# Output projection moved into the token tiles of the spectral layer, tokens handed over in SBUF

## Chip, cores and metric

The kernel runs on one core of a Trainium2 chip. Its time is the device time of the whole program in microseconds. The kernel before takes 1611.79 us, the median of three runs (1611.19 to 1612.21).

## What is computed

x is [2048, 576] in float32. Four layers follow one another, each with a layer norm over the features and a residual: attention (A), spectral (B), A, B.

```
def _A_ref(x, wqkv, wo):          # H = 32 heads of 18, window W = 256
    q, k, v = qkv[0], qkv[1], qkv[2]              # from x @ wqkv
    scores = einsum("bhqd,bhkd->bhqk", q, k) * (Dh ** -0.5)
    p = softmax(where(0 <= i - j < W, scores, -1e9))
    return merge_heads(p @ v) @ wo                # the output projection
def _B_ref(x, w_r, w_i):
    return irfft2(rfft2(x) * (w_r + 1j * w_i))
x = x + _A_ref(_layernorm(x), wqkv, wo)
x = x + _B_ref(_layernorm(x), w_r, w_i)           # and both once more
```

## The kernel before, in words

The program is written out in the order in which each engine runs it; there is no scheduler. Every engine, and SP as the main DMA queue, goes through its own instructions in order and waits on semaphores. Numbers are kept as a high and a low part, so that a product is three matmuls (high by high, low by high, high by low).

**Layer A** (`layer_a`, L433) has a first stage over 16 token tiles (norm, transposes, v) and a second one over 128 steps: 8 groups of 4 heads by 16 query tiles. In step t the scores are multiplied (E, L661), ACT takes the exponentials (L662), POOL masks them (L664, L667), and two steps later the products with v go to a PSUM bank U (`pv`, L677). After four query tiles U is copied by ACT (L682), and `norm` (L684) transposes it, divides by the row sums on DVE (L690, L692) and stores 72 features of 512 tokens to the DRAM tensor `o_d` (L693, SP).

The output projection is done in the same loop, from step OB = 120 on, one tile of 128 neighbouring tokens a step: `o_load` (L729) reads o and x, `o_tail` (L733) splits the last 64 features on POOL, `o_turn` (L736) makes five transposes and splits the result on ACT and DVE, `o_unit` (L748) makes 28 matmuls of 288 columns (14 steps by two halves), adds x on DVE, stores the new token rows (L760), takes the mean and variance on DVE (L764 to L766) and stores those as well (`mv_d`, L767). Tiles 0 to 6 lie between the last attention steps, the rest follow. `o_room` (L712) puts the weights `wo` and these tiles into the space of the attention's inputs, which are done by then.

**Layer B** (`layer_b`, L98) begins by reading `mv_d` back (L122) and taking 1/sqrt for all tokens (L136 to L138), makes an identity, and loads the tokens in pairs of tiles (`ld`, L111) and the constants dc and gc (L118, L119). A token tile is strided here: tile n2 holds the tokens 16 p + n2 for the partitions p. The first stage is `pipe(NT, ...)` (L239), which staggers these functions over the 16 tiles: `f0` (L166: xn on ACT, its even and odd parts eo and the small tile tl on POOL), `f1` (L189: six transposes into the PSUM tile tp, split into et by ACT and DVE), `f2` (L202: 14 matmuls of 290 columns with dc, PSUM tile pf, split into yh and yl), `f3` (L217: 12 matmuls with gc, PSUM tile pz, copied to ye and stored to the DRAM tensor yd). In a step f1 is for the tile after that of f2, and f3 for the tile before. Loads for later stages go out on the way: fc, m2 and w in `pre` (L155), ic (128 x 12 x 290) and ga (128 x 1024) in f0 of tile 8 (L168, L169).

The next stage reads yd crosswise, a group g at a time (`g0`, L241), so it needs all of the first stage. The first group is put together in SBUF from the stored tiles and, for the last three tiles (FD = 13), from ye directly (L228 to L235). `g1m` (L253, matmuls p) and `g2` (L271, matmuls pq) follow, then a second exchange, and the last stage (`i0`, `i1`, `i2`, from L304; matmuls pi and po), which reads the tokens again for the residual and stores the layer's result.

Of the kernel before, what the change touches and what calls it, by code (L numbers as in the profile page):

```python
# [17 lines left out]
NF = 290  # L18
# [79 lines left out]
def layer_b(tc, src, dst, mv_d, dc_d, ic_d, fc_d, gc_d, ga_d, m2_d, w_d, dram):  # L98
# [6 lines left out]
    with tc.tile_pool(name="bc", bufs=1) as cp, tc.tile_pool(name="bw", bufs=2) as wp, \  # L105
# [4 lines left out]

        def ld(n2, h):  # L111
            if n2 % 2 == 0:
                x = wp.tile([128, 2, D], F32, tag="x", name=f"x{n2}", bufs=4)
# [3 lines left out]
            if n2 == 0 and not ys:  # L117
                nc.sync.dma_start(dc.bitcast(F32), dc_d.bitcast(F32))  # L118
                nc.sync.dma_start(gc.rearrange("p a j b c -> p (a j b c)").bitcast(F32), gc_d.bitcast(F32))  # L119

        mv = cp.tile([128, NT, 2], F32, name="mv")
        nc.sync.dma_start(mv.rearrange("p a b -> p (a b)"), mv_d.rearrange("(p n) e -> p (n e)", n=NT))  # L122
        eps = cp.tile([128, 1], F32, name="eps"); V.memset(eps, 1e-5)

        A.activation(cp.tile([128, 1], F32, name="se"), eps, AF.Sqrt)
        ident = cp.tile([128, 128], F32, name="ident")
        make_identity(nc, ident)
        dc = cp.tile([128, 10, NF], F32R, name="dc")
        gc = cp.tile([128, 2, 2, 2, 128], F32R, name="gc")
        ga = cp.tile([128, 2, 2, 256], F32R, name="ga")  # L130
        fc = cp.tile([128, 16, 2, 2, 64], F32, name="fc")
        m2 = cp.tile([128, 16, 2, 128], F32, name="m2")
        ic = cp.tile([128, 12, NF], F32R, name="ic")
        rs = cp.tile([128, NT], F32, name="rs")
        nb = cp.tile([128, NT], F32, name="nb")
        A.activation(rs, mv[:, :, 1], AF.Sqrt, bias=eps)  # L136
        V.reciprocal(rs, rs)
        V.scalar_tensor_tensor(nb, mv[:, :, 0], -1.0, rs, op0=ALU.mult, op1=ALU.mult)  # L138
        zs, eos = [], []
# [13 lines left out]
        NW = 7  # L153
# [12 lines left out]
        def f0(n2, h):  # L166
            if n2 == 8:
                nc.sync.dma_start(ic.bitcast(F32), ic_d.bitcast(F32))  # L168
                nc.sync.dma_start(ga.rearrange("p a j c -> p (a j c)").bitcast(F32), ga_d.bitcast(F32))  # L169
            if n2 == 6:  # L170
                for j in range(3):
                    z = cp.tile([128, 2, 2, 354], F32R, name=f"zs{j}")
                    V.memset(z.bitcast(F32)[:, :, :, 289:320], 0.0)
                    zs.append(z)
            x = xs[n2]
            xn = wp.tile([128, D], F32, tag="ta", name=f"xn{n2}", bufs=3)
            A.activation(xn, x, AF.Identity, bias=nb[:, n2:n2 + 1], scale=rs[:, n2:n2 + 1])
            eo = h["eo"] = eos[n2 % 4]
            P.tensor_add(eo[:, 0, 1:288], xn[:, 1:288], xn[:, 575:288:-1])
            A.copy(eo[:, 0, 0:289:288], xn[:, 0:289:288])  # L180
            (V if n2 < 2 else P).tensor_sub(eo[:, 1, 0:287], xn[:, 1:288], xn[:, 575:288:-1])

            tl = h["tl"] = wp.tile([128, 2, 3, 33], F32, tag="td", name=f"tl{n2}", bufs=3)
            e = eo[:, :, 256:289]
            P.tensor_copy(tl[:, :, 0].bitcast(F32R), e)
            P.tensor_copy(tl[:, :, 2].bitcast(F32R), e)
            P.tensor_sub(tl[:, :, 1].bitcast(F32R), e, tl[:, :, 0])
# [14 lines left out]
        def f2(n2, h):  # L202
            ps = pp.tile([128, 2, 512], F32, tag="mm", name=f"pf{n2}", bufs=3)
            et = h["et"]
            for c in range(2):
# [3 lines left out]
                for q, (si, mi) in enumerate(seq):  # L209
                    T.matmul(o, et[:, c, si], dc[:, b + mi], start=q == 0, stop=False)  # L210
                T.matmul(o, et[0:99, c, 4], dc[0:99, b + 4], start=False, stop=True)
# [5 lines left out]
        def f3(n2, h):  # L217
# [10 lines left out]
            if n2 == FD:  # L228
                y = wp.tile([128, 2, 2, NF], F32, tag="x", name="y0", bufs=4)
                nc.sync.dma_start(y[0:8 * FD].rearrange("p a c f -> p a (c f)"), yd[0][0:2, 0:FD].rearrange("a n i f -> (n i) a f"))  # L230
                for q in range(2):
                    ys[q] = y[:, q]
# [6 lines left out]
        pipe(NT, [(0, ld), (5, lambda n2, h: n2 or f2(n2, h)), (4, f1), (5, lambda n2, h: n2 and f2(n2, h)), (6, f3), (2, f0)])  # L239

        def g0(g, h):  # L241
            if g % 2 == 0 and g not in ys:
                y = wp.tile([128, 2, 2, NF], F32, tag="x", name=f"y{g}", bufs=4)
                nc.sync.dma_start(y.rearrange("p a c f -> p a (c f)"), yd[0][g:g + 2].rearrange("a n i f -> (n i) a f"))
                for q in range(2):
                    ys[g + q] = y[:, q]
# [6 lines left out]
        def g1m(g, h):  # L253
# [6 lines left out]
            p1 = wp.tile([128, 2, NF], F32, tag="tw", name=f"p1_{g}")  # L260
# [10 lines left out]
        def g2(g, h):  # L271
# [9 lines left out]
            if g == FD:  # L281
                for n2 in range(2):
                    y = ys["i", n2] = wp.tile([128, 2, NF], F32, tag="y", name=f"yi{n2}", bufs=4)
# [10 lines left out]
        pipe(16, [(0, g0), (9, g2), (7, g1m), (2, gw)])  # L294

        def ly(n2, h):
# [4 lines left out]
            y = h["y"] = wp.tile([128, 2, NF], F32, tag="y", name=f"yi{n2}", bufs=4)  # L301
# [32 lines left out]
        def i2(n2, h):  # L334
# [14 lines left out]
            bs = wp.tile([128, NF], F32, tag="td", name=f"bs{n2}", bufs=3)  # L349
# [10 lines left out]
NQ = 8  # L360
# [72 lines left out]
def layer_a(tc, src, dst, mv_d, wqk_d, wv_d, wo_d, dram, copy, wvs, second):  # L433
# [5 lines left out]
    o_d = dram.tile([S, D], F32, name="o_d")  # L439
    with ExitStack() as ctx:  # L440
# [115 lines left out]
        with ExitStack() as c2:  # L556
# [127 lines left out]
            def norm(n, c):  # L684
# [8 lines left out]
                nc.sync.dma_start(o_d[c * 512:(c + 1) * 512, 72 * n:72 * n + 72].rearrange("(a p) e -> p a e", a=4), o)  # L693
# [16 lines left out]
            ob = {}  # L710

            def o_room():  # L712
                for r, parts in ((bp.tile([128, 5 * S], F32R, tag="xh", name="oroom"), (("wh", 1, 5 * D), ("wl", 1, 5 * D), ("oT", 3, 9 * 128))),
                                 (bp.tile([128, 4 * S], F32, tag="xl", name="ofree"), (("x", 6, D), ("o", 4, D), ("tl", 4, 128)))):
                    at = 0
                    for nm, n, w in parts:
                        ob[nm] = [r[:, at + k * w:at + k * w + w] for k in range(n)]
                        at += n * w
                ob["raw"] = r[:, 0:5 * D]
                for a, b in ((0, 2), (2, 5)):  # L720
                    nc.sync.dma_start(ob["raw"][:, a * D:b * D], wo_d[:, a * D:b * D])

            def o_split(k):
                c = slice(k * D, k * D + D)
                raw = ob["raw"][:, c]
                A.copy(ob["wh"][0][:, c], raw)
                P.tensor_sub(ob["wl"][0][:, c], raw, ob["wh"][0][:, c].bitcast(F32))

            def o_load(u):  # L729
                nc.sync.dma_start(ob["o"][u % 4], o_d[u * 128:(u + 1) * 128])  # L730
                nc.sync.dma_start(ob["x"][u % 6], src[u * 128:(u + 1) * 128])

            def o_tail(u):  # L733
                tail_split(nc, ob["tl"][u % 4], ob["o"][u % 4][:, 512:576])

            def o_turn(u):  # L736
                o, tl = ob["o"][u % 4], ob["tl"][u % 4]
                oT = ob["oT"][u % 3]
                tp = pp.tile([128, 512], F32, tag="S", name=f"tpa{u}", bufs=3)
                for kt in range(4):  # L740
                    T.transpose(tp[:, kt * 128:kt * 128 + 128], o[:, kt * 128:kt * 128 + 128], ident)
                tq = pp.tile([128, 512], F32, tag="S", name=f"tpb{u}", bufs=3)
                T.transpose(tq[:, 0:128], tl, ident)
                A.copy(oT[:, 0:512], tp)
                V.tensor_sub(oT[:, 512:1024], tp, oT[:, 0:512].bitcast(F32))
                A.copy(oT[:, 1024:1152], tq[:, 0:128])

            def o_unit(u):  # L748
                oT = ob["oT"][u % 3]
                ps = [pp.tile([128, 512], F32, tag="E" if u > 4 and u % 2 else "pj", name=f"ops{u}_{n}", bufs=2) for n in range(2)]  # L750
                ks = k_steps()
                for i, (wk, p, xk) in enumerate(ks):
                    w = ob["wh" if p == "h" else "wl"][0]
                    for n in range(2):
                        T.matmul(ps[n][:, 0:288], oT[:, xk * 128:xk * 128 + 128], w[:, wk * D + n * 288:wk * D + n * 288 + 288],  # L755
                                 start=i == 0, stop=i == len(ks) - 1)
                x = ob["x"][u % 6]
                for n in range(2):
                    V.tensor_add(x[:, n * 288:n * 288 + 288], x[:, n * 288:n * 288 + 288], ps[n][:, 0:288])
                nc.sync.dma_start(dst[u * 128:(u + 1) * 128], x)  # L760

                st = wp.tile([128, 2, 6], F32, tag="st", name=f"ost{u}", bufs=2)
# [88 lines left out]
```

## Time and profile before

| | |
|---|---|
| time of the profiled execution | 1608.87 us |
| its span | 1607.2 us |
| mean TensorE clock granted | 0.97 |
| matmul windows at 590 to 603 us: PE busy | 0.42 of 13 us |
| DMA moved | 277.96 MB, mean 173 GB/s |

How it is read: PE is TensorE's matmuls, PEld its weight loads, DVE is VectorE, ACT ScalarE, POOL GpSimd, SP the DMA queue of SyncE. A line such as L755 is a line of the kernel before. Rows of groups have the operation, output and inputs by the program's names, the count, then busy time, the mean in ns, and the idle time before with what ended it. Rows of the timeline have start, length, engine, line and operation. The chain of work is followed back from the last instruction. PEclk is the share of the full clock that TensorE was granted. Two layers of each kind run, so each hand-over from A to B occurs twice, at about 590 and 1390 us.

### The profile page before, as it was taken

How to read it: one execution, taken by the hardware profiler on the slowest of the kernel's cores; microseconds unless marked ns; L12 is line 12 of the kernel's file. 1: busy time of each engine (PE TensorE's matmuls, PEld its weight loads, DVE VectorE, ACT ScalarE, POOL GpSimd, SP SyncE). 2: the span in 40 equal slices, each digit the busy share in tenths (PEclk: the TensorE clock that was granted, in tenths of full speed). 3: DMA queues.
4: the chain of work that ended last, by engine and by line, in shares of the span. 5: the costliest groups of instructions: out<-in, count | busy, mean ns of one | idle time of the engine just before them, and what ended most of it. 6: DMA issues, size and time to landing. Idle time of an engine off the chain costs nothing.

```text
span 1607.2 us, 38259 instructions
## 1 busy us (share of the span) xinstructions
PE 1507.2 (94%) x13872; PEld 1146.1 (71%) x13872; DVE 961.1 (60%) x3047; ACT 811.0 (50%) x1876; POOL 623.8 (39%) x1030
## 2 busy tenths in 40 slices
PE   7999999999999969998979999999999999799898
PEld 7975666666656968848979756666666569698498
DVE  4337777777774444456743377777777745444566
ACT  5524666666667115424445246666666671153244
POOL 2172334444445105352411723444343451153534
PEclk9999999999999988998979999999999999899989
DMA  6656446455543856866474564454434438678673
GB/s 194 181 180 200 145 149 184 151 167 151 155 133 98 165 160 239 285 216 215 149 231 116 177 204 149 142 156 140 140 120 148 135 100 168 180 246 277 209 227 135
DMA packets 189385, 277.96 MB, mean 173 GB/s; under 512 B 87566, under 2 KB 88590, under 8 KB 188174
## 3 DMA queue, kind: packets, MB, share of 16 engines
q1 hardware_dynamic: 180878, 255.54, 53.1%
q10 hardware_dynamic: 7680, 15.59, 2.9%
q0 software_dynamic: 640, 4.39, 1.0%
q8 instruction: 111, 1.82, 0.5%
q14 instruction: 76, 0.62, 0.1%
HBM read 176.47 MB, written 102.32 MB: 173 GB/s over the span
## 4 chain that ended last, share of the span: by engine, by line
PE 83%; DMA 4%; POOL 2%; ACT 2%; DVE 2%; issue 1%; SPq 1%; POOLq 0%; ACTq 0%; DVEq 0%
PE pj L588 15%; PE E L661 14%; PE U L677 12%; PE ops L755 7%; PE S L629 6%; PE pi L322 5%; PE vps L546 4%; PE pf L210 4%; PE pz L223 3%; PE po L343 3%; PE tpo L687 2%; PE p L258 1%; DMA yd<-ze 1%; PE pq L277 1%; PE po L347 1%
## 5 line engine op out<-in xcount | busy, mean ns | idle before, releaser
L631 DVE CUSTOM_DVE_ANT_0 jk<-S,mask 128x384 bf16<-128x384 f32 (+2 forms) x1024 | 500.2, 529 | 151.3 <-PE S L629 139.0
L662 ACT ACTIVATE P<-E 128x384 f32<-128x384 f32 (+2 forms) x1024 | 426.1, 471 | 216.8 <-PE E L661 189.7
L664 POOL TENSOR_SCALAR_AFFINE_SELECT P<-P 128x512 f32<-128x512 f32 x256 | 162.3, 634 | 464.4 <-ACT P L662 446.1
L661 PE MATMUL E<-qs,ks 64*128 64x384 f32 (+2 forms) x1024 | 267.5, 431 | 10.7 <-ACT P L662 10.1
L661 PEld LDWEIGHTS E<-qs,ks 64*128 64x128 f32 x1024 | 129.2, 184 | 152.7 <-ACT P L662 89.6
L629 PE MATMUL S<-ks,qs 63*128 63x384 f32 (+2 forms) x1024 | 228.1, 350 | 0.3 <-DVE m L631 0.2
L677 PE MATMUL U<-P,vq 128*19 128x128 f32 x5760 | 208.6, 276 | 0.1
L677 PEld LDWEIGHTS U<-P,vq 128*19 128x19 f32 x5760 | 136.5, 98 | 56.5 <-issue 53.6
L588 PE MATMUL pj<-xh,wqh 128*128 128x512 f32 x360 | 153.5, 426 | 1.7 <-ACT vt L550 1.7
L629 PEld LDWEIGHTS S<-ks,qs 63*128 63x128 f32 x1024 | 130.7, 186 | 24.8 <-DVE m L631 13.2
L667 POOL TENSOR_SCALAR_AFFINE_SELECT P<-P 128x512 f32<-128x512 f32 x224 | 142.0, 634 | 0.0
L755 PE MATMUL ops<-oroom 128*128 128x288 f32 x896 | 127.4, 299 | 3.2 <-DVE o L692 3.2
L588 PE MATMUL pj<-xh,wql 128*128 128x512 f32 x360 | 123.9, 418 | 0.1
L755 PEld LDWEIGHTS ops<-oroom 128*128 128x128 f32 x896 | 120.4, 189 | 3.9 <-issue 3.0
L588 PE MATMUL pj<-xl,wqh 128*128 128x512 f32 x288 | 119.0, 413 | 0.0
L322 PE MATMUL pi<-ga,zs 128*128 128x256 f32 (+1 forms) x576 | 78.7, 293 | 15.2 <-ACT zs L307 15.2
L592 DVE TENSOR_TENSOR sg<-pj,sg 128x512 fp32r<-128x512 f32 x72 | 49.8, 692 | 70.2 <-ACT sg L591 67.5
L588 PEld LDWEIGHTS pj<-xh,wqh 128*128 128x128 f32 x360 | 67.5, 188 | 33.4 <-issue 21.8
L322 PEld LDWEIGHTS pi<-ga,zs 128*128 128x128 f32 (+1 forms) x576 | 74.8, 192 | 16.7 <-ACT zs L307 16.1
L631 DVE DVE_READ_ACCUMULATOR2_ANT m<- 128x1 f32 x1024 | 84.9, 83 | 0.0
L588 PEld LDWEIGHTS pj<-xh,wql 128*128 128x128 f32 x360 | 64.0, 188 | 27.2 <-issue 17.7
L591 ACT CAST sg<-pj 128x512 fp32r<-128x512 f32 x72 | 42.3, 587 | 80.1 <-PE pj L588 54.1
(137 smaller groups left out, 2471.2 us busy)
## 6 DMA issues: line engine op xcount, KB each, us to landing
qk_d<-sg SPq DMA_DIRECT2D x56, 512.0 KB
qs<-qk_d SPq DMA_DIRECT2D x384, 72.0 KB
ks<-qk_d SPq DMA_DIRECT2D x384, 72.0 KB
x<-x SPq DMA_DIRECT2D x32, 576.0 KB
v_d<-vt SPq DMA_DIRECT2D x32, 304.0 KB
vq<-v_d SPq DMA_DIRECT2D x16, 608.0 KB
yd<-ye SPq DMA_DIRECT2D x32, 290.0 KB
wt<-in_w SPq DMA_DIRECT2D x16, 580.0 KB
```

What stands on the lines that cost most here:

```text
L210: T.matmul(o, et[:, c, si], dc[:, b + mi], start=q == 0, stop=False)
L322: T.matmul(o, z[:, sl, c, lo:lo + m], mo, start=k == 0, stop=k == 5)
L546: T.matmul(ps[:, n, 0:288], xT(xk, c), w[:, wk, n * 288:(n + 1) * 288], start=i == 0, stop=i == len(ks) - 1)
L588: T.matmul(box["ps"], w[:, wk], xT(xk, cs), start=s == 0, stop=s == len(ks) - 1)
L629: T.matmul(ps[:, 0:N], q[b:b + 63, pair, i * 128:i * 128 + 128], k[b:b + 63, pair, lo:hi], start=True, stop=True)
L631: V.tensor_tensor_reduce(out=jk[:, 0:N], in0=ps[:, 0:N], in1=mask[:, 384 - N:384], scale=1.0, scalar=-3e38, op0=ALU.add, op1=ALU.max, accu ...
L661: T.matmul(ps[:, 0:nq], k[b:b + 64, pair, j * 128:j * 128 + 128], q[b:b + 64, pair, j * 128:j * 128 + nq], start=True, stop=True)
L662: A.activation(p[:, hl_, 0:nq], ps[:, 0:nq], AF.Exp, scale=SC)
L664: P.affine_select(out=p[:, :, 0:128], in_=p[:, :, 0:128], pattern=[[0, 4], [1, 128]], compare_op=ALU.is_ge, fill=0.0, base=0, channel_mult ...
L667: P.affine_select(out=p[:, :, 256:384], in_=p[:, :, 256:384], pattern=[[0, 4], [-1, 128]], compare_op=ALU.is_gt, fill=0.0, base=0, channel ...
L677: T.matmul(U[32 * h:32 * h + 19, (i % 4) * 128:(i % 4) * 128 + 128], vts[n][:, j, h], pt[n, j][:, h, (i - j) * 128:(i - j) * 128 + 128], s ...
L755: T.matmul(ps[n][:, 0:288], oT[:, xk * 128:xk * 128 + 128], w[:, wk * D + n * 288:wk * D + n * 288 + 288], start=i == 0, stop=i == len(ks) ...
```

## The change

The output projection leaves layer A's loop. A new class `Out` holds its pieces, and they are called from layer A's end and from layer B, which now runs inside layer A's SBUF space (`spectral`). The projection's token tiles take layer B's stride, so each tile's new rows stay in SBUF (`self.x`), are also stored for the later residual, and go straight into `f0`. Mean, variance and 1/sqrt are taken tile by tile (`sums`, `stats`).

Since a strided tile has tokens from the whole sequence, no tile is complete before the last head group is. So o is stored in two tensors: 448 features, and the last 128 (`o7_d`), of which the weights' rows are put in accordance. `early` makes the 11 of 14 steps that need the 448, `late` the last 3. At the end of layer A the early steps of tiles 0 to 2 stand around the last `norm`; then come the late ones. In layer B a turn of the loop has the whole projection of tile t + 4, f1 of t, f3 of t - 1, f0 of t + 4, f2 of t, and load and transposes of tile t + 6 and t + 7.

```diff
-            for t in range(-LEAD, OB + 5 + NT):
+            out = Out(nc, ident, eps, bp, ov, o7v, srcv, dstv, wo_d, dc_d, gc_d)
+            for t in range(-LEAD, NX + 2):
...
-                for lag, f in ((4, o_turn), (5, o_unit), (3, o_tail), (0, o_load)):
-                    if 0 <= t - OB - lag < NT:
-                        f(t - OB - lag)
+                if t - OB in (0, 1, 2):
+                    out.load(t - OB)
+                if t == OB + 3:
+                    out.consts()
...
+                if t - OB - 5 in (0, 1, 2):
+                    u = t - OB - 5
+                    out.turn(u, pp.tile([128, 512], F32, tag="pj", name=f"tpa{u}", bufs=2), V)
+                    if u < 2:
+                        out.load(u + 3)
+                if t == NX:
+                    A.activation(wp.tile([128, 1], F32, name="se", bufs=1), eps, AF.Sqrt)
+            out.last(slice(0, 96))
+            out.early(0, [...], slice(0, 4))
+            norm(NQ - 1, 3)
+            out.last(slice(96, 128))
+            out.early(0, None, slice(4, 11))
+            out.early(1, [...])
+            out.early(2, [...])
+            out.turn(3, U, A)
+            out.tail(4)
+            for f in (out.turn_last, out.split_last):
+                for u in range(3):
+                    f(u, tp[:, 128 * u:128 * u + 128])
+            for u in range(3):
+                out.late(u)
...
+            out.turn(4, pp.tile([128, 512], F32, tag="E", name="tpa4", bufs=2), A)
+        spectral(dst, out.dcs, out.gc, ident, out.rh, out.rl, out)
```

`consts` loads dc (as five tiles) and gc into space of layer A; `last` reads `o7_d` (first the tokens of partitions 0 to 95, then the rest); `turn` makes a tile's four transposes and, in layer B, the fifth. `unit` is `early` and `late` together, with the adds and the store of x; `ahead(u)` loads tile u + 1, splits its tail and turns tile u. In layer B:

```diff
-        pipe(NT, [(0, ld), (5, lambda n2, h: n2 or f2(n2, h)), (4, f1), (5, lambda n2, h: n2 and f2(n2, h)), (6, f3), (2, f0)])
+        f0(0, hs[0])
+        out.load(5)
+        norm(1)
+        out.tail(5)
+        out.unit(3, pp)
+        f1(0, hs[0])
+        norm(2)
+        out.unit(4, pp)
+        f2(0, hs[0])
+        out.ahead(5, pp)
+        norm(3)
+        for t in range(1, NT - 4):
+            u = t + 4
+            out.unit(u, pp)
+            f1(t, hs[t])
+            if t == 1:
+                f3(0, hs[0])
+                out.ahead(6, pp)
+                norm(4)
+            out.sums(u)
+            if t > 1:
+                f3(t - 1, hs[t - 1])
+            f0(u, hs[u])
+            f2(t, hs[t])
+            out.ahead(u + 2, pp)
+        f1(NT - 4, hs[NT - 4])
+        for t in range(NT - 4, NT + 1):
+            for v, f in ((t, f2), (t + 1, f1), (t - 1, f3)):
+                if v < NT:
+                    f(v, hs[v])
```

(`norm(u)` here is `sums` and `f0` of tile u.) Since layer A's space stays in use, layer B's tiles for y, x, ic, ga and zs are laid into it. The loads of ic and ga move from f0 of tile 8 to f3 of tile 13, behind the load of the first group's stored part:

```diff
+                nc.sync.dma_start(y_tile(0)[0:8 * FD]..., yd[0][0:2, 0:FD]...)
+                for z in zs:
+                    V.memset(z.bitcast(F32)[:, :, :, 289:320], 0.0)
+                nc.sync.dma_start(ic..., ic_d...)
+                nc.sync.dma_start(ga..., ga_d...)
             if n2 >= FD:
                 for g in range(2):
                     (nc.scalar if n2 == NT - 1 else nc.sync).dma_start(ys[g][8 * n2:8 * n2 + 8]..., yef[8 * g:8 * g + 8])
             nc.sync.dma_start(yd[0][:, n2], yef)
```

Six pairs of w instead of seven are loaded ahead of the next stage (NW), and in that stage `g0` comes last in a step instead of first.

More of the change, by code (lines that the diff above doesn't have):

```diff
@@ L116, in ld @@
                     xs[n2 + q] = x[:, q]
[L117 to L130, printed above, removed]
         fc = cp.tile([128, 16, 2, 2, 64], F32, name="fc")
         m2 = cp.tile([128, 16, 2, 128], F32, name="m2")
[L133 to L139, printed above, removed]
+        eos = []
         for j in range(4):
@@ L434, in layer_a @@
+def layer_a(tc, src, dst, wqk_d, wv_d, wo_d, dc_d, gc_d, dram, copy, wvs, second, spectral):
     nc = tc.nc
@@ L736, in o_turn @@
[L736 to L762, printed above, removed]
-                mv = wp.tile([128, 2], F32, tag="mv", name=f"omv{u}", bufs=2)
-                for k in range(2):
-                    V.bn_stats(st[:, k], x[:, k * 288:(k + 1) * 288])
-                V.bn_aggr(mv, st.rearrange("p a b -> p (a b)"))
-                nc.sync.dma_start(mv_d[u * 128:(u + 1) * 128], mv)
```

226 lines of the change are left out of this document (166 added, 60 removed).

## The prediction

> **What bounds the kernel now.** I read the page first, then the chain that ended last, then the timeline and the windows around the place where the attention layer hands over to the spectral layer. The page says that the matmul engine is the bound nearly everywhere:
>
> ```profile
> PE 1507.2 (94%) x13872; PEld 1146.1 (71%) x13872; DVE 961.1 (60%) x3047; ACT 811.0 (50%) x1876; POOL 623.8 (39%) x1030
> ```
>
> So what counts is where PE stands still or runs at a lower clock. The chain in order of time (start, length, what) shows it for the two hand-overs, at 583 to 621 and at 1385 to 1417:
>
> ```profile
> 574.42 3.73 PE ops L755 x28
> 578.69 3.73 PE ops L755 x28
> 582.96 7.34 PE ops L755 x55
> 592.15 3.91 DMA mv_d<-omv
> 596.76 4.20 DMA x<-x
> 605.85 2.06 PE pf L210 x6
> 621.27 1.61 PE pz L223 x12
> 625.43 1.61 PE pz L223 x12
> ...
> 674.72 3.29 PE pz L223 x24
> ...
> 1385.10 3.61 PE ops L755 x27
> ...
> 1474.59 3.29 PE pz L223 x24
> ```
>
> The output projection runs at 578.69 - 574.42 = 4.27 us a token tile, the first spectral stage at 625.43 - 621.27 = 4.16, both with PE full. Between them PE waits for two round trips through DRAM in series: the last means (592.15), then the tokens read back (596.76). The timeline has the length of the gap (the bracket is idle time and what ended it), in both layers:
>
> ```profile
> 603.11 0.48 PE L193 MATMUL tp<-ident,eo 128*128 128x128 f32 x1 [12.69 <-POOL eo L179]
> 1404.34 0.47 PE L193 MATMUL tp<-ident,eo 128*128 128x128 f32 x1 [11.78 <-POOL eo L179]
> ```
>
> and four windows have the clock after it (PE busy first; the third number from the end is PEclk, then DMA share and GB/s):
>
> ```profile
> 590.00:603.00 13.00, 0.42 (x4) 0.19 (x2) 2.81 (x14) 3.64 (x7) 1.50 (x3) 0.64 0.48 172
> 603.00:612.00 9.00, 6.97 (x26) 5.77 (x26) 2.24 (x4) 3.38 (x7) 4.57 (x13) 0.57 0.66 273
> 612.00:617.00 5.00, 4.15 (x23) 4.18 (x24) 0.99 (x2) 2.55 (x6) 2.24 (x5) 0.71 0.00 2
> 617.00:622.00 5.00, 5.00 (x38) 5.00 (x38) 2.23 (x4) 3.01 (x7) 2.24 (x5) 0.95 0.23 46
> ```
>
> After 12.7 us of idleness the clock stands near 0.6 until about 617. The hand-over thus costs its idle time and a slow start.
>
> **The change, part by part.** I compare the time from one point, the first output-projection transposes, to the last pz matmul. These rows give the point and the rest of the attention behind it:
>
> ```profile
> 511.89 0.66 PE L741 MATMUL tpa<-ident,ofree 128*128 128x128 f32 x4
> 513.09 0.85 PE L677 MATMUL U<-P,vq 128*19 128x128 f32 x24
> ...
> 1314.02 0.66 PE L741 MATMUL tpa<-ident,ofree 128*128 128x128 f32 x4
> ```
>
> Before: 674.72 + 3.29 - 511.89 = 166.1 us in layer 1 and 1474.59 + 3.29 - 1314.02 = 163.9 in layer 2.
>
> *Matmul work.* It stays: 28 matmuls and 5 transposes a tile in the projection, the same 32 in the spectral stage. 16 x 4.27 = 68.3, 16 x 4.16 = 66.6, and the attention left at 511.89: five groups of U at 0.8, two norms and the last scores, about 7. Sum 142. So the kernel before loses 24 us in layer 1 and 22 in layer 2.
>
> *Removed.* The mean and token round trips, the identity, the Sqrt table load and dc/gc loads at the hand-over; all stand in the gap, none elsewhere.
>
> *Added or moved, in the order of PE's queue.* (a) The token tiles are now strided, so no projection can end before the last head group is stored. PE does 11 of 14 steps of tiles 0 to 2 (58 matmuls behind norm, 7.7 us) while the last 128 features go to DRAM and back. From 511.89 come three tiles' transposes (0.54 each, 4.27 - 3.73), the five U groups, a norm and the scores, about 8.5 us in all: the last U ends near 520.4. With the copy of U, norm's transposes and DVE the last features are stored from about 523, and PE, busy with the 58 matmuls and a tile's transposes, wants them back at 530.3. The nearest row for a store's landing is the queue's own wait (us in total, times, longest), and from the chain comes the longest store of the next stage:
>
> ```profile
> SPq L730 <- DMA o_d<-o: 9.4, 5, 2.6
> 692.33 7.81 DMA yd<-ze
> ```
>
> Two legs of about 3 us land near 529; two legs at the longest row, 7.8, would land near 538. I take the former (the same kind of store; the dc and gc loads, 2 MB issued from about 511, should be drained by 519), stall 0, and keep 8 us a layer as the other end. A wait for the copy of U costs about 0.5, the split of the last features ahead of the first late step about 0.9.
>
> (b) The norm of tile 0 is a serial chain ahead of the first spectral transposes. Its durations, five from the timeline, one more for the small copies, and two groups (busy, mean ns of one):
>
> ```profile
> 590.33 0.82 DVE L759 TENSOR_TENSOR ofree<-ofree,ops 128x288 f32<-128x288 f32 x2 [1.94 <-PE ops L755]
> 591.07 0.81 DVE L765 BATCH_NORM_STATS2 ost<-ofree 128x6 f32<-128x288 f32 x2
> 591.91 0.21 DVE L766 BATCH_NORM_AGGREGATE omv<-ost 128x2 f32<-128x12 f32 x1
> 601.05 0.87 ACT L177 ACTIVATE xn<-x,nb,rs 128x576 f32<-128x576 f32 x1 [2.75 <-DMA x<-x]
> 602.00 1.06 POOL L179 TENSOR_TENSOR eo<-xn 128x287 f32<-128x287 f32 x1 [4.88 <-ACT xn L177]
> 603.12 0.38 POOL L185 CAST tl<-eo 128x66 fp32r<-128x66 f32 x1
> ...
> L512 ACT ACTIVATE rs<-mv,eps 128x1 f32<-128x1 f32 x32 | 10.2, 319 | 17.4 <-DVE mv L509 9.0 <-DMA wvh<-wvs 8.3
> L512 ACT ACT_TABLE_LOAD x1 | 1.3, 1283 | 0.8 <-PEq L844 0.8
> ```
>
> On DVE the adds of tiles 0, 1 and 2 (0.82 each), the sums (1.02), splits of 128 and 384 columns (0.2 and 0.5, estimated from 0.41 for 288) and the scale stand in a row: 5.0 us. Then come ACT's 0.9, POOL's 1.06 and three small copies, about 0.9: 7.9 us after tile 0's last step. PE has the late steps of tiles 1 and 2 (0.8 each), transposes and unit 3 until 6.4: stall 1.5. In turn t = 1 the load of tile 7 goes out 1.7 us behind f3 (after a copy and a store's issue), lands at 4.3 and is split by 4.9, where PE has only a turn and an f2, 2.5 us: stall 2.4; and 0.4 for the transpose bank that f1 and the turn share. Sqrt now comes once a tile between copies; 32 Sqrt of layer A's first stage made one table load, so no reload is charged.
>
> [...] The row above shows no reload between Sqrt and copies; if it did, 32 loads of 1.28 us on ACT would still have room beside PE.
>
> (c) The loop: unit (28 matmuls), f1, f3 of the tile before, f2, next turn: 4.27 + 4.16 = 8.43 us on PE. f1 now stands only one group (1.61) ahead of its f2. What must happen between, from the timeline, and the group of the longest DVE pass:
>
> ```profile
> 619.41 0.59 ACT L198 CAST et<-tp 128x512 fp32r<-128x512 f32 x1 [1.03 <-PE tp L195]
> 620.03 0.69 DVE L199 TENSOR_TENSOR et<-tp,et 128x512 fp32r<-128x512 f32 x1 [0.51 <-ACT et L198]
> 620.76 0.37 ACT L200 CAST et<-tp 99x256 fp32r<-99x256 f32 x1 [0.76 <-DVE et L199]
> ...
> L215 DVE TENSOR_TENSOR yl<-pf,yh 128x580 fp32r<-128x580 f32 x32 | 24.4, 762 | 47.9 <-ACT yh L214 47.9
> ```
>
> After f1's end at about 619.2 the high part is there at +0.8, the low at +1.5, the tail at +1.9; f2 needs them at +1.6, +1.9 and +2.4. It fits. From f1's start, in the queues' order: et until 2.2, sums 3.2, Sqrt 3.5, the copy of pz 4.0, scale 4.3, xn 5.2, yh about 6.0, yl (0.76) 6.9, the turn's splits 7.6. The bank is free at 7.6 of 8.43, so the loop stays with PE, at nothing extra; without that cover it costs what the third rival says. The POOL tail split waits for a load, but the next thing behind it on POOL is needed only some 4 us later. In the drain f2 once follows f1 at once: 0.8 for the high part and 0.6 for the low, 1.4.
>
> Stalls 0.5 + 0.9 + 1.5 + 0.4 + 2.4 + 1.4 = 7.1; 142 + 7 = 149. The stage ends 17 us earlier in layer 1 and 15 in layer 2: **32 us**.
>
> [...]
>
> (d) The loads of ic and ga move from the eighth tile to the fourteenth, on SP's queue ahead of the last three stores of the exchange, and one more w is loaded in the next stage. Rows: the size from the page, SP's and PE's timeline at the exchange of before, and a window with the fastest DMA near it.
>
> ```profile
> ic<-icr SPq DMA_DIRECT2D x2, 1740.0 KB
> ...
> 678.51 1.26 SPq L236 DMA_DIRECT2D yd<-ye  x2
> 682.76 17.30 SPq L244 DMA_DIRECT2D y<-yd  x7
> 681.98 3.83 PE L258 MATMUL p<-y,fc 128*64 128x290 f32 x16 [3.98 <-DMA y<-ye]
> ...
> 650.00:655.00 5.00, 5.00 (x40) 5.00 (x40) 2.22 (x3) 3.23 (x7) 2.34 (x6) 1.00 1.05 414
> ```
>
> ic and ga are 2.3 MB (ga's 512 KB by its shape), 5.6 us at 414 GB/s. They are issued about 4 us ahead of the last pz, so the pieces behind them land about 5 us after it instead of 4, and the next y is read about 2 us later, where 5 us of p and pq work cover most. With the added w I take 2 us a layer. The bounds are below 0 (fewer loads earlier leave the queue emptier; 1 us gained) and 11 (2.9 MB in full, at 260 GB/s).
>
> **Sum.** 32 - 2 x 2 = 28 us. The profiled execution took 1608.87 us (span 1607.2), so about 1581; the median of the runs shown is 1611.79, 2.9 above it, and I set the forecast against that: **1584 us**.
>
> **Rivals.**
> - *The round trip shows.* The last features come back at the slow end, (a): 8 us a layer, 28 - 16 = 12 gained, 1600. For it speaks the 7.81 row, against it that no burst of loads runs beside it. Chance 0.12.
> - *The exchange pays.* ic and ga delay the whole next stage, (d): 9 us more a layer, 28 - 18 = 10 gained, 1602. For it: that stage waited for DMA before already (3.98 and 7.81 above). Chance 0.15.
>
> [...]
>
> - *Slower: the loop isn't PE's.* f1's copies come too late for f2 because ACT or DVE is held by another tile's norm or splits in the same in-order queue. It costs up to the whole et chain, 1.9 us, in each of 11 turns in two layers: 42 us, 14 slower, 1626. It decides from 28 / 22 = 1.3 us a turn. For it: the chain's cover falls from a full stage to 1.61 us. Against it: the slack counted above, and DVE 60% and ACT 50% busy. Chance 0.09.
> - *It doesn't do what it says.* The projection that used to fill the attention's last steps is missing there, and the hand-over only moves ahead of the last head group: a gap of its old size stands at the late steps, within 3 us of 1612. Against it: 58 matmuls are left to fill it. Chance 0.05.
>
> **How the numbers follow.** Forecast 0.59; its own range 1576 to 1592. The range 1574 to 1603 holds it and the first two rivals, and leaves 0.14 out. Faster by over 0.2% (3.2 us, about what a measurement of this kernel can tell from none): 0.59 + 0.12 + 0.15 = 0.86. Same 0.05, slower 0.09.
>
> **What would show it.** Right: no PE gap over 3 us between the last U and the last pz, PEclk near 1.0 there, 8.4 us from one unit to the next, the last pz about 661, and about 1448 in layer 2 (1477.9 less 15 net and 15), pi starting 50 to 54 us after it. Wrong: turns of over 9.7 us, a DMA releaser ahead of the late steps, a clock under 0.8 after the attention, or the next stage longer by over 5 us.

## The result, and the profile after

The changed kernel took 1614.59 us (median of 20 runs, 1610.22 to 1618.52); the kernel before, run beside it, 1609.98 us (20 runs, 1602.28 to 1613.43). The ratio is 1.0031, 95% interval [1.0020, 1.0043]: **4.6 us slower, where 28 us faster was forecast.** The profiled execution of the changed kernel has a span of 1614.0 us.

PE is as full as before, in share. The page's line of the changed kernel:

```profile
PE 1514.2 (94%) x13872; PEld 1145.7 (71%) x13872; DVE 976.2 (60%) x3141; ACT 813.7 (50%) x1900; POOL 626.0 (39%) x1028
```

The same 13872 matmuls are busy 7 us longer, and PE stands idle for 100 us in either kernel, so other waits and, in places, a lower clock (0.77 and 0.70 in two windows below; the mean granted is 0.97 in both kernels) must have taken what the hand-over gave. To find where, I cut each layer at three points that both kernels have: the transposes of the last norm but two (tpo), the last pz and the first pi. First the kernel before, from PE's timeline (start, length, what; in brackets the idle time ahead and what ended it); its last pz stand in the prediction:

```profile
509.48 0.65 PE L687 MATMUL tpo<-ident,us 128*128 128x128 f32 x4
730.49 7.60 PE L322 MATMUL pi<-ga,zs 128*128 128x256 f32 x36 [7.68 <-ACT zs L307]
1311.61 0.66 PE L687 MATMUL tpo<-ident,us 128*128 128x128 f32 x4
1530.51 1.81 PE L322 MATMUL pi<-ga,zs 128*128 128x256 f32 x5 [7.47 <-ACT zs L307]
```

The same view of the changed kernel:

```profile
507.90 0.66 PE L840 MATMUL tpo<-ident,us 128*128 128x128 f32 x4
669.30 0.30 PE L209 MATMUL pz<-yh,oroom 128*128 128x290 f32 x1
729.45 7.33 PE L340 MATMUL pi<-oroom 128*128 128x256 f32 x36 [7.53 <-ACT oroom L325]
1316.58 0.66 PE L840 MATMUL tpo<-ident,us 128*128 128x128 f32 x4
1477.06 0.29 PE L209 MATMUL pz<-yh,oroom 128*128 128x290 f32 x1
1535.40 1.81 PE L340 MATMUL pi<-oroom 128*128 128x256 f32 x5 [8.10 <-ACT oroom L325]
```

| us, layer 1 / layer 2 | before | after | difference | forecast |
|---|---|---|---|---|
| tpo to last pz (hand-over, first spectral stage) | 168.5 / 166.3 | 161.7 / 160.8 | -6.8 / -5.5 | -17 / -15 |
| last pz to first pi (exchange, next stage) | 52.5 / 52.6 | 59.9 / 58.1 | +7.4 / +5.4 | +2 / +2 |
| first pi to last po (last stage) | 71.6 / 71.0 | 73.1 / 73.0 | +1.5 / +2.0 | 0 / 0 |

Differences are taken before rounding. The sum is +4 us, and the medians differ by 4.6. The gap at the hand-over did go (from 12.7 us idle to none over 2.9), but it gave 12 us instead of 32, and 16 us were lost behind it. The two profiled spans differ by 6.8. The rest lies in the attention: from the last po of layer 1 to layer 2's tpo it takes 509.5 us before and 514.0 after. That stretch takes 508.6 to 514.2 us over all the profiled kernels of this document, in no order of their edits, so I don't put it down to the change.

**The hand-over** in the changed kernel, layer 1, PE's timeline:

```profile
532.48 0.52 PE L518 MATMUL tpl<-ident,ofree 128*128 128x128 f32 x3 [2.78 <-DMA ofree<-o_d]
539.71 3.99 PE L529 MATMUL ops<-oroom 128*128 128x288 f32 x28 [1.27 <-DVE oroom L512]
551.20 0.53 PE L529 MATMUL ops<-oroom 128*128 128x288 f32 x2 [0.68 <-ACT oroom L511]
562.87 0.52 PE L506 MATMUL tpo<-ident,ofree 128*128 128x128 f32 x3 [2.07 <-DMA ofree<-o_d]
563.75 5.49 PE L529 MATMUL ops<-oroom 128*128 128x288 f32 x28
573.73 3.97 PE L529 MATMUL ops<-oroom 128*128 128x288 f32 x28
582.20 3.96 PE L529 MATMUL ops<-oroom 128*128 128x288 f32 x28
650.91 0.54 PE L196 MATMUL pf<-dc,et 128*128 128x290 f32 x2 [1.29 <-ACT et L184]
```

From 573.73 on the loop is what was forecast: 582.20 - 573.73 = 8.47 us a turn, PE with no gap. Ahead of it stand four gaps, behind it one in the drain (650.91), and unit(6) at 563.75 takes 5.49 us for the same 28 matmuls (in layer 2, behind a gap of 2.06 us, it takes 3.96, with 1.00 granted from 1370 to 1375). Two windows show why (clock third from the end):

```profile
535.00:540.00 5.00, 3.73 (x20) 3.48 (x21) 4.37 (x18) 1.30 (x4) 0.00 (x0) 0.77 0.39 148
565.00:570.00 5.00, 5.00 (x31) 5.00 (x30) 2.25 (x5) 1.79 (x6) 3.43 (x11) 0.70 0.02 8
```

The chain that ended last has the DMAs behind the first gap:

```profile
518.78 4.21 DMA o_d<-o
523.44 5.64 DMA o_d<-o
529.10 3.13 DMA ofree<-o_d
```

The last head group is stored by quarters of the tokens. The third quarter's store, issued at 518.78, takes 4.21 us; the fourth's goes out on the same queue behind the 786 KB read of the first three, takes 5.64, and the read of the fourth another 3.13.

**The exchange.** SP's queue, and what SP waited for (total, times, longest):

```profile
664.76 0.34 SPq L218 DMA_DIRECT2D oroom<-icr  x1
669.35 4.46 SPq L222 DMA_DIRECT2D ofree<-ye  x2
675.75 1.27 SPq L223 DMA_DIRECT2D yd<-ye  x2
680.06 9.45 SPq L264 DMA_DIRECT2D ofree<-yd  x5
```

```profile
SPq L222 <- DMA oroom<-icr: 3.2, 1, 3.2
```

Of the two pieces of tile 14 (L222) the second stood still until ic had landed, and the read of the next y (L264) went out at 680.06, 10.5 us after the last pz; in the kernel before it is 682.76 - 678.01 = 4.75.

### The profile page after: what moved, and what is told of

Its sections match the earlier page's. It is cut to its first block, busy times and chain, and to the rows that moved or that the text cites. A ratio compares the mean times of both kernels' runs of the same rounds, so it can differ in the third digit from the quotient of the medians.

```text
span 1614.0 us, 38199 instructions
## 1 busy us (share of the span) xinstructions
PE 1514.2 (94%) x13872; PEld 1145.7 (71%) x13872; DVE 976.2 (60%) x3141; ACT 813.7 (50%) x1900; POOL 626.0 (39%) x1028
## 4 chain that ended last, share of the span: by engine, by line
PE 79%; DMA 8%; ACT 3%; DVE 2%; issue 1%; SPq 1%; POOL 1%; POOLq 0%; ACTq 0%; DVEq 0%
PE pj L741 17%; PE E L814 14%; PE U L830 12%; PE S L782 7%; PE ops L529 6%; PE vps L699 4%; PE pi L340 3%; PE pz L209 3%; PE po L361 3%; PE pf L196 3%; DMA yd<-ze 3%; PE tpo L840 2%; DMA o_d<-o 1%; ACT P L815 1%; PE po L365 1%
## 5 line engine op out<-in xcount | busy, mean ns | idle before, releaser
L814 PE MATMUL E<-qs,ks 64*128 64x384 f32 (+2 forms) x1024 | 269.1, 433 | 12.3 <-ACT P L815 11.5
L830 PEld LDWEIGHTS U<-P,vq 128*19 128x19 f32 x5760 | 137.2, 99 | 57.2 <-issue 53.9
L529 PE MATMUL ops<-oroom 128*128 128x288 f32 x784 | 114.7, 303 | 5.1 <-DVE oroom L512 3.0
L529 PEld LDWEIGHTS ops<-oroom 128*128 128x128 f32 x784 | 107.1, 192 | 7.4 <-DVE oroom L512 4.0
L340 PE MATMUL pi<-oroom 128*128 128x256 f32 (+1 forms) x576 | 78.5, 293 | 15.6 <-ACT oroom L325 15.6
L340 PEld LDWEIGHTS pi<-oroom 128*128 128x128 f32 (+1 forms) x576 | 74.6, 191 | 17.2 <-ACT oroom L325 16.5
L165 POOL TENSOR_TENSOR eo<-xn 128x287 f32<-128x287 f32 x32 | 26.1, 817 | 146.5 <-ACT xn L163 135.4
```

Source lines behind the costliest of these rows:

```text
L340: T.matmul(o, z[:, sl, c, lo:lo + m], mo, start=k == 0, stop=k == 5)
L529: self.nc.tensor.matmul(self.ps[u][n][:, 0:288], x, self.w[p][:, wk * D + n * 288:wk * D + n * 288 + 288], start=first and i == 0, stop=la ...
L814: T.matmul(ps[:, 0:nq], k[b:b + 64, pair, j * 128:j * 128 + 128], q[b:b + 64, pair, j * 128:j * 128 + nq], start=True, stop=True)
L830: T.matmul(U[32 * h:32 * h + 19, (i % 4) * 128:(i % 4) * 128 + 128], vts[n][:, j, h], pt[n, j][:, h, (i - j) * 128:(i - j) * 128 + 128], s ...
```

## The experiments

The theory after this reading: two losses stand apart. The first stage is held by waits at its start, some with a slow clock behind them (0.77 and 0.70 in the windows above); the exchange is held by ic and ga. Rivals: the later w, traffic on the DMA engines, or waits that hide one another. Every kernel was timed 5 to 12 times beside the kernel before, whose median was 1607.4 to 1610.7 us from one session to the next; so kernels of different sessions are compared by their ratios. The changed kernel's own is 1.0031 [1.0020, 1.0043].

| run | median, us | ratio to before, 95% interval |
|---|---|---|
| x1_icga_early | 1603.33 | 0.9955 [0.9937, 0.9973] |
| b1_icga_late | 1622.27 | 1.0066 [1.0044, 1.0088] |
| x12_icga_pool | 1603.67 | 0.9968 [0.9952, 0.9984] |
| b2_nw6 | 1610.11 | 1.0015 [1.0001, 1.0029] |
| x2_o7_part | 1608.90 | 0.9993 [0.9975, 1.0011] |
| x9_o7_turn4 | 1610.51 | 1.0013 [0.9993, 1.0034] |
| x3_load7 | 1618.29 | 1.0050 [1.0034, 1.0066] |
| x8_load7_norm4 | 1611.73 | 1.0023 [1.0007, 1.0038] |
| x5_i0 | 1610.81 | 1.0019 [1.0001, 1.0036] |
| x6_all | 1593.48 | 0.9904 [0.9882, 0.9925] |
| x10_no_turn4 | 1591.10 | 0.9896 [0.9874, 0.9918] |
| x11_more | 1591.43 | 0.9891 [0.9871, 0.9911] |

### The exchange: four runs

x1_icga_early, on the changed kernel:

```diff
+            if n2 == 10:   # f3(10), behind the last unit
+                nc.sync.dma_start(ic...); nc.sync.dma_start(ga...)
             if n2 == FD:
...
-                nc.sync.dma_start(ic...); nc.sync.dma_start(ga...)
```

> The changed kernel, with the loads of ic and ga moved from f3(13) to f3(10), the first place behind the last projection unit. Theory (the loads stand on SP's queue and in the rings ahead of the last pieces and stores of the exchange): last pz to first pi falls from 59.8 and 58.0 us to about 53, the 4.46 us issue of the pieces (SPq) shrinks to about 1.3, the time falls by 10 to 13 us to about 1603. Rival (the one w that is loaded later, or the new order of the next stage's first instructions, makes that stage longer): last pz to first pi stays at 58 to 60 and the time at 1612 to 1616.

b1_icga_late, on the kernel before:

```diff
-            if n2 == 8:
-                nc.sync.dma_start(ic...); nc.sync.dma_start(ga...)
...
             if n2 == FD:
+                nc.sync.dma_start(ic...); nc.sync.dma_start(ga...)
```

> The kernel before, with that one part of the change alone: ic and ga loaded in f3(13) instead of f3(8). Theory: last pz to first pi grows from 52.5 to 57 to 60 in both layers and the time rises by 10 to 13 us against the kernel before, to about 1621. Rival (the later w, the order): it stays near 52.5, time within 3 us of the kernel before.

Both came out as the theory has it. Last pz to first pi is 53.3 and 54.1 us in x1 (59.9 and 58.1 in the changed kernel) and 59.6 and 58.0 in b1 (52.5 and 52.6 in the kernel before). SP's queue in x1, to be held against the rows above:

```profile
667.79 1.30 SPq L223 DMA_DIRECT2D ofree<-ye  x2
673.85 12.35 SPq L265 DMA_DIRECT2D ofree<-yd  x6
```

The pieces take 1.30 us instead of 4.46, and the next y is read 5.2 us after the last pz (668.38 + 0.30). b1 alone makes the kernel before slower by 11.5 us, as much as x1 gives back. So the loads' new place is shown to be the loss, from both sides.

b2_nw6, on the kernel before: `NW = 7` becomes `NW = 6`.

> The kernel before, with only six of the eight w pairs loaded in the first stage instead of seven: the other half of step (d). Theory (the late ic and ga are the whole loss of the next stage): last pz to first pi stays within 1 us of 52.5 and the time within 2 us of the kernel before. Rival (the later w costs part of it): 54 to 56 us, 3 to 6 us slower.

Last pz to first pi stays at 52.4 and 52.5 us, so the later w is not it. The time is 2.7 us over that of the kernel before, a little above what was expected, with an interval that barely leaves out no change; that stage does not show it, and where it lies is open.

x12_icga_pool, on the changed kernel: at the same place, `nc.sync.dma_start` becomes `nc.gpsimd.dma_start` for ic and ga.

> The changed kernel, with ic and ga loaded at the same place (f3(13)) but issued by POOL on its own queue instead of by SP. It asks what delays the exchange. If it is SP's queue (SP itself stood 3.2 us until ic had landed, and the pieces and stores behind it left late): the pieces leave within 1.5 us, last pz to first pi about 54, the time near 1603, as when the loads are moved earlier. If it is the traffic (2.3 MB on the same 16 DMA engines at that moment): SP's wait goes, yet the y tiles come as late as in the changed kernel, 57 to 60 us, about 1612 to 1615.

54.6 and 53.9 us, 1603.67: the time and the stage of x1. SP's queue in this run, and POOL's issue of ic (first and last start in us, after the durations in ns):

```profile
666.56 1.29 SPq L222 DMA_DIRECT2D ofree<-ye  x2
672.09 13.64 SPq L264 DMA_DIRECT2D ofree<-yd  x6
```

```profile
L218 POOL DMA_DIRECT2D oroom<-icr x2: 592/595/598, 650.1 to 1454.4; - x2
```

SP no longer stands, but the same place in the program is not the same moment. POOL reaches it earlier and issues ic at 650.1, 17.4 us ahead of the end of the last pz (667.45); in the changed kernel SP issues it at 664.76, 4.8 us ahead. ic and ga land 8.4 and 9.2 us after their issue, so they are in by about 660, before any piece goes out. As in x1, the loads then stand neither ahead of the pieces on SP's queue nor beside them on the DMA engines, so this run can't tell **SP's queue from the traffic**. Other rows speak for a part of the traffic: the last tile's pieces go out on ACT's queue, and the chain has one of them, in x12 and then in the changed kernel:

```profile
668.27 2.93 DMA ofree<-ye
670.43 5.30 DMA ofree<-ye
```

The piece takes 2.93 us without the loads in flight (2.95 in the kernel before) and 5.30 beside them (5.47 in b1), on a queue that the loads are not on, and SP's next store (L223, at 675.75) goes out when it has landed. SP's own 3.2 us for ic are the other part in sight; how the loss divides between the two is open. A run in which POOL holds the loads back until SP would issue them was not made. The rings that the expectations of x1 and x2 name are my guess at how a transfer is held up; no run shows them.

### The last features' round trip: x2_o7_part

```diff
-            out.last(slice(0, 96))
+            out.last(slice(0, 96), slice(0, 5))      # tiles 0 to 4
...
             norm(NQ - 1, 3)
-            out.last(slice(96, 128))
+            out.last(slice(96, 128), slice(0, 5))
+            out.last(slice(0, 128), slice(5, NT))
```

> The changed kernel, with the last features read back for tiles 0 to 4 first (245 KB instead of 786 KB ahead of the last store) and for the other eleven behind it. Theory (the last store waits in the rings behind the big read): its landing falls from 5.6 to about 4 us, PE's gap ahead of the last features' transposes from 2.8 to under 1 us, and the clock after it stays near 1, so 3 to 4 us a layer, 1614.6 to about 1608. Rival (a store and a read take 4.2 and 3.1 us whatever runs beside them): the gap stays over 2 us and the time within 2 us of 1614.6.

As the theory has it: 1608.90 us, and the interval lies below that of the changed kernel. SP's queue and PE's timeline in x2:

```profile
522.42 0.38 SPq L850 DMA_DIRECT2D o_d<-o  x1
525.52 0.78 SPq L497 DMA_DIRECT2D ofree<-o_d  x2
```

```profile
528.26 0.49 PE L518 MATMUL tpl<-ident,ofree 128*128 128x128 f32 x3
535.73 3.98 PE L529 MATMUL ops<-oroom 128*128 128x288 f32 x28 [1.27 <-DVE oroom L512]
558.88 0.52 PE L506 MATMUL tpo<-ident,ofree 128*128 128x128 f32 x3 [2.08 <-DMA ofree<-o_d]
559.75 3.96 PE L529 MATMUL ops<-oroom 128*128 128x288 f32 x28
```

The last store lands in 525.52 - 522.42 = 3.1 us, the figure that I had forecast, and the 2.78 us gap is gone; three of about 0.5 us stand behind it. The smaller read (245 KB instead of 786) leaves fewer bytes both ahead of the store on its queue and in flight beside it; which of the two counts is open here too. Note the last two rows: the 2.08 us gap ahead of tile 7 is still there, but here the unit behind it takes 3.96 us and not 5.49.

### Turn t = 1: x3_load7 and x8_load7_norm4

```diff
         norm(3)
+        out.load(7)              # x3 and x8; ahead(6) no longer loads it
...
-                norm(4)          # x8: from turn t = 1
+        norm(4)                  # x8: to here, ahead of out.load(7)
```

> The changed kernel, with tile 7's tokens requested right behind norm(3) instead of in turn t = 1 behind the store of f3(0). Theory: the 2.07 us gap ahead of tile 7's transposes goes, and with it the slow unit behind it (5.49 us instead of 3.96): 3.5 us a layer, 1614.6 to about 1607.5. Rival (the time is lost again at the next wait, the load then being late for another reason: the buffer is freed by tile 2's norm and store): gap of 1.5 to 2 us stays, time within 2 us.

This was a miss: 1618.29 us, no gain on the changed kernel. The load's gap is gone, but PE, then ACT, in x3:

```profile
563.73 3.96 PE L530 MATMUL ops<-oroom 128*128 128x288 f32 x28
570.34 0.47 PE L179 MATMUL tp<-ident,eo 128*128 128x128 f32 x1 [2.65 <-DVE oroom L525]
```

```profile
566.77 0.87 ACT L163 ACTIVATE xn<-ofree 128x576 f32<-128x576 f32 x1 [0.55 <-POOL eo L165]
567.77 0.64 ACT L200 CAST yh<-pf 128x580 fp32r<-128x580 f32 x1
568.30 0.59 ACT L512 CAST oroom<-tpo 128x512 fp32r<-128x512 f32 x1
```

Tile 7's transposes are done at 564, but ACT copies them only at 568.30, behind two norms (the second is the first row) and a yh, and until then the next f1 may not have the bank. The load had hidden that wait.

> The changed kernel, with tile 7's tokens requested behind norm(3) as in the run that moved this load alone, and norm(4) moved ahead of unit(5). Theory (in turn t = 1 two norms stand in ACT's and DVE's queues ahead of turn(7)'s copies, so that the shared transpose bank is freed late, and the load was only the wait that showed): both the 2.07 us gap ahead of tile 7's transposes and the 2.65 us gap ahead of the next f1 go, the unit between them runs at about 4 us, and the first stage is 3 us a layer shorter than in the changed kernel, about 1608 to 1610. Rival (the bank is late for another reason, the POOL operations of the norms): a gap of over 1.5 us stays there and the time at 1614 or above.

With norm(4) out of the way, PE in x8:

```profile
557.62 0.55 PE L507 MATMUL tpo<-ident,ofree 128*128 128x128 f32 x3 [0.94 <-ACT et L186]
565.58 0.33 PE L179 MATMUL tp<-ident,eo 128*128 128x128 f32 x1 [0.82 <-DVE oroom L525]
```

The 2.07 and 2.65 us are replaced by 0.94 and 0.82, so it is shown that the norms ahead of turn(7)'s copies held the bank. The time did not follow: 1611.73 us misses the expected 1608 to 1610, and its interval overlaps that of the changed kernel. In the profiled execution tpo to last pz is 162.9 and 161.2 us, no shorter than 161.7 and 160.8: layer 1 has a 3.87 us gap at the last features instead of 2.78, and layer 2 a unit(3) of 5.50 us.

### Turn(4): x9_o7_turn4

On top of x2's edit (tail(4) also goes ahead of turn(3)):

```diff
             out.turn(3, U, A)
+            out.turn(4, U, A)
...
-            out.turn(4, pp.tile([128, 512], F32, tag="E", name="tpa4", bufs=2), A)
```

> The changed kernel with the split read of the last features (as in the run of that alone, 1608.9) and turn(4) moved ahead of the late steps, into the bank that turn(3) used. Theory (unit(3) and turn(4) wait for turn(4)'s copies and for a shared bank): the 0.53 us gap ahead of turn(4) and the 1.27 us gap ahead of unit(3) go, so first transposes to last pz are 1.5 us a layer shorter than in that run, about 1606. Rival: unit(3)'s start is set by the norm or by late(2)'s adds; the gap stays within 0.5 us and so does the time.

1610.51 us against 1608.90 for x2 alone, with intervals that overlap: no gain, as the rival has it. PE in x9:

```profile
528.93 0.55 PE L506 MATMUL U<-ident,ofree 128*128 128x128 f32 x3 [1.27 <-DVE oroom L512]
536.00 3.95 PE L529 MATMUL ops<-oroom 128*128 128x288 f32 x28 [1.56 <-DVE ofree L564]
```

The gap moved to where turn(4) now stands, and unit(3) waits as long as before, for what ends on DVE in front of L564, most likely late(2)'s adds on banks that the unit reuses (argued, not tried).

### The last stage: x5_i0

```diff
             A.copy(z[:, 0, :, 0:DF], h["y"][:, :, 0:DF])
+            A.copy(z[:, 0, :, 320:353], zf[:, 0, :, 256:289])
             V.tensor_sub(z[:, 1, :, 0:DF], h["y"][:, :, 0:DF], zf[:, 0, :, 0:DF])
-            A.copy(z[:, 0, :, 320:353], zf[:, 0, :, 256:289])
```

> The changed kernel, with two instructions of the last stage's i0 in the other order: ACT's small copy inside zs ahead of DVE's subtraction. Theory (zs is now cut from one flat tile, so that copy waits for the subtraction, holds ACT, and the zh copies of the next tile come late): the pi cadence falls from 4.37 to about 4.27 us, first pi to last po from 73.1 to about 71.5 us, 1614.6 to about 1611.5. Rival (the 0.09 us a tile come from the place of the operands in memory): cadence and time unchanged.

The cadence is as the theory has it. The row of ACT's waits in the changed kernel, and of PE in both (the changed kernel first):

```profile
ACT oroom L327 <- DVE oroom L326: 21.8, 14, 1.6
```

```profile
743.59 2.27 PE L340 MATMUL pi<-oroom 128*128 128x256 f32 x18
747.96 2.28 PE L340 MATMUL pi<-oroom 128*128 128x256 f32 x18
```

```profile
740.90 2.28 PE L340 MATMUL pi<-oroom 128*128 128x256 f32 x18
745.17 2.28 PE L340 MATMUL pi<-oroom 128*128 128x256 f32 x18
```

4.37 us a tile becomes 4.27, and first pi to last po 71.1 and 71.9 us instead of 73.1 and 73.0. The time alone would not show it: by the ratios the gain is 2 us, and the intervals overlap. But that stage takes 70.9 to 72.3 us in both layers of the four kernels that have the swap (x5, x6, x10, x11), and 72.4 to 73.6 in the changed kernel and its six versions without it. In the kernel before, where zs was a tile of its own, ACT has no wait of this kind in its list. The two instructions touch different columns (one reads 0 to 288, the other writes 320 to 352); that their flattened ranges overlap is my explanation of the wait, and the swap shows only that it was not needed.

### All together: x6_all, x10_no_turn4, x11_more

x6 has the edits of x1, x2, x8, x9 and x5; x10 the same without turn(4)'s; x11 adds to x10 that turn(5) stands ahead of f2(0), and f1(12) ahead of f2(11).

> The changed kernel with all edits: ic and ga in f3(10), the last features read in two parts, tile 7's load and norm(4) earlier, turn(4) ahead of the late steps, and i0's order. Theory (separate waits, each on PE's path): the gains add up, 11 + 5.5 + 4 + 3 + 3 us, 1614.6 to about 1588, and ahead of the kernel before by 1.3%. Rival (the waits hide one another): less than 20 us in all, 1595 or above.

> The kernel with all edits but one: turn(4) back behind the late steps, where the changed kernel has it. Theory (moved ahead, turn(4) waited for turn(3)'s copies and held the last features' transposes, and unit(3) waited for late(2)'s adds in any case, so that edit gave nothing or a little loss): first transposes to last pz 150 to 153 us instead of 154.8 and 153.4, the time 1593.5 or up to 4 us less. Rival (the edit was worth its 1.5 us a layer and only the clock hid it): 1594 to 1597.

> The same, with two more waits taken away: turn(5) ahead of f2(0) instead of directly ahead of its unit, and f1(12) ahead of f2(11) instead of directly ahead of its f2. Theory: the gaps of 0.68 + 0.24 and of 1.29 + 0.36 us go in both layers, 2 to 2.5 us a layer, 4 to 5 us below the run beside it. Rival (the transposes now wait for the shared bank): within 1.5 us of it.

x6 takes 1593.48 us, 21 us less than the changed kernel and 20 by the ratios: less than the 26.5 that were expected, and too near the rival's 20 to decide. By the ratios the single gains add up to 18. x10 takes 1591.10 and x11 1591.43; the intervals of all three lie on each other, so neither turn(4)'s place nor x11's two edits can be told from nothing. In x10 first transposes to last pz are 155.2 and 152.2 us, so the expected 150 to 153 came in one layer. x10 is 0.9896 [0.9874, 0.9918] of the kernel before: **the change with the edits of x1, x2, x8 and x5 is 1% faster than the kernel before**, and 1.3% faster than the changed kernel. What x11 removed in gaps, a longer wait (0.96 us in x10, the second row) and in layer 2 the clock (the first row, with 0.66 granted from 1330 to 1335; 3.98 us in x10, with 1.00) took:

```profile
1330.87 5.50 PE L532 MATMUL ops<-oroom 128*128 128x288 f32 x28 [1.27 <-DVE oroom L515]
555.74 0.55 PE L509 MATMUL tpo<-ident,ofree 128*128 128x128 f32 x3 [1.85 <-ACT et L186]
```

## Why the prediction was wrong

Forecast and measured stages differ by 32 us in all: 10.2 and 9.5 from tpo to the last pz, 5.4 and 3.4 in the exchange, 1.5 and 2.0 in the last stage.

**(d) failed, the largest single term.** I charged the loads' new place 2 us a layer. Measured: 7.4 and 5.4. I had worked out how long 2.3 MB take at 414 GB/s and priced too low what they hold up. I had listed what stands behind them (the last three stores) and then said that they "land about 5 us after it instead of 4" and that the next y is read 2 us later. In layer 1 SP stood 3.2 us for ic, the last piece landed 6.1 us after the last pz instead of 3.8, and the next y was asked for 10.5 us after it instead of 4.75. x1 and b1 show that the place does it; how much of it is SP's queue and how much the traffic stays open (x12). The rival "the exchange pays" had the loss in the right stage, at 9 us more a layer where 5.4 and 3.4 came, and a chance of 0.15. The other half of the step, the added w, was right at nothing in that stage (b2).

**(a) failed.** I took two legs of 3 us and stall 0. The last store landed in 3.1 us only where 245 KB were read ahead of it (x2); here a 786 KB read of the same features stood there, and it took 5.64. The stall was 2.78 us and 0.36 for the split, inside my bounds of 0 and 8. I also took the dc and gc loads to be drained by 519; from 520 to 521 the DMA engines still moved 341 GB/s, and the third quarter's store took 4.21 us beside that. The other reasons I gave held: PE was busy with the 58 matmuls, and the copy of U was covered.

**(b) was near in size and half right in cause.** Forecast 1.5 at the first spectral transposes, for the norm of tile 0; measured no gap there and 1.27 one unit earlier, at unit(3), whose releaser was not settled (x9), so that this size is luck. Forecast 2.4 for tile 7's load; measured 2.07 + 0.16. But I took that load for the end of it: behind it ACT's and DVE's queues held turn(7)'s copies for longer (x3). It is the third rival's mechanism, in one turn instead of eleven. Forecast 0.4 for the transpose bank; 0.68 + 0.24 at unit(5) and 0.19 in t = 1. No Sqrt reload came, as forecast: the 32 Sqrt of layer B (L560) have no table load, and ACT's table loads are five, of 1.28 us each, in either kernel.

**(c) was right.** 8.47 us a turn, PE-bound, and 1.29 + 0.36 = 1.65 in the drain against 1.4.

**The clock was left out.** I put it at nothing, a term that no run shows: the windows of the kernel before have the clock after 12.7 us of idleness (0.57), and behind stalls of 2.8 us and less the runs had it lowered in some places (0.57 and 0.70, below) and at 1.00 in others. The stalls from the last U to the last pz sum to 9.4 us in layer 1 against 7.1 forecast, and with them came about 3.3 us of slow matmuls: 1.5 at 563.75 (0.70 granted from 565 to 570) and about 1.8 at the late steps (from 533.35 to 537 they came at 0.24 us and not at 0.13, with 0.57 granted). The forecast's time from the last U to the last pz, 140.6 us, was 149.8; 2.3 of the 9.2 are stalls, 3.3 clock, and some 3.6 I can't assign to single rows; their cause stays open. In layer 2 the unit behind tile 7's gap kept its clock (3.96 us, with 1.00 granted), so the clock's price differs from layer to layer.

**The starting point.** I measured from the first projection transposes. In the changed kernel they come one attention step later (four groups of U behind them instead of five), so part of the 9 us that this pair of points shows, 157.0 us against 166.1, is no gain; from the norm's transposes it is 6.8.

**Not in the sum at all:** the last stage, +1.5 and +2.0 us, by an order of two instructions that the change did not touch but whose tile it replaced (x5).

## What to carry to other kernels

Price a load by what it holds up, not by its bytes alone: 2.3 MB just ahead of a few small transfers cost about 11 us in two layers, against the same loads some 20 us earlier (x1, b1). A move to another engine's queue can move the load in time too (x12: issued at 650.1 and not at 664.76), so look at when it is issued before calling the queue the cause. Where a large idle gap is filled with work, look at the small waits that it leaves, and expect that one may hide another: taking away tile 7's alone gave nothing (x3: 1618.29 us against 1614.59). A tile that is cut out of a larger one should be looked over for waits between parts that do not meet (x5; argued).

## What the runs showed of the hardware that was not expected

Matmuls were slow behind gaps of 1.27 us and less, but not each time. In x10 the same unit stands behind the same gaps (0.52, 0.45, 0.53, then 1.27 us, within 7 us) in both layers, and only one is slow:

```profile
537.21 5.52 PE L531 MATMUL ops<-oroom 128*128 128x288 f32 x28 [1.27 <-DVE oroom L514]
1333.79 3.98 PE L531 MATMUL ops<-oroom 128*128 128x288 f32 x28 [1.27 <-DVE oroom L514]
```

In layer 1 the granted clock is 0.73 from 535 to 540 and 0.93 from 540 to 545; in layer 2 it is 1.00 from 1330 to 1340. So 1.5 us hang on something besides the lengths of these gaps. What that is was not tried.
